# Sums of squares on eight rows, with root and reciprocal there and a spread over DRAM

## The chip, the core and the metric

The kernel runs on one core of a Trainium2 chip. A core has five engines, each with an instruction queue of its own that it works off in order: TensorE (PE in the profile; PEld is its weight load, which can run beside a matmul), VectorE (DVE), ScalarE (ACT), GpSimd (POOL) and SyncE (SP), which here only issues DMAs. Matmul results go to PSUM, from which DVE or ACT must fetch them. The metric is the device time of one execution in microseconds; lower is better.

## The reference

A linear attention is followed by two gated feed-forward layers, all in fp32:

```python
def _attn_ref(q, k, v, g_norm):                 # (4, 8, 576, 64) each
    kv = np.einsum('bhsd,bhse->bhde', k, v)
    out = np.einsum('bhsd,bhde->bhse', q, kv)
    rms = np.sqrt(np.mean(out * out, axis=-1, keepdims=True) + 1e-06)
    return out / rms * g_norm

x = attn_out.transpose(0, 2, 1, 3).reshape(2304, 512)
x = (1 / (1 + np.exp(-(x @ w_gate))) * (x @ w_val)) @ w_out    # d_ff 1536
h = x @ w_in2                                                   # d_ff 2048
out = (np.maximum(h, 0) + np.log1p(np.exp(-np.abs(h)))) @ w_out2
```

The root mean square is taken per token and head, over the 64 values of that head.

## The kernel before

Every fp32 product is made of three matmuls over a high and a low half of each operand (`mm3`); `split` makes the halves, the high one on ACT (L66) and the low one on DVE (L69). The instruction order is written out by hand, engine by engine.

The 2304 tokens are cut into five tiles (512, 512, 384, 384, 512). The first feed-forward layer runs over 60 iterations n, twelve per tile; layer two follows. One iteration of TensorE is a chain of twelve matmuls `ps_g`, one of twelve `ps_v`, and one of twelve `yacc` for the iteration before. Between the chains there are named places, in this order: `A` (after `ps_g`), `a`, `bg`, then after `ps_v` `B`, `b`, `end`, then after `yacc` `C`, `c`, `late`. Matmuls of other work go to the capital places, what fetches their results to the small ones. On ACT and DVE the iteration has `sigmoid` after `A`, the product `gated` (L509, DVE, into `sg`) between `B` and `b`, and its halves `ghl`. `gated` also frees the PSUM bank of `ps_v`.

The attention of tiles u = 2, 3, 4 is woven into the iterations of tile u - 1. A tile is worked in pieces of at most 256 tokens; there are seven: 128 and 256 tokens wide (u = 2), 160, 160 and 64 (u = 3), 256 and 256 (u = 4). A piece has four pairs of heads, hp = 0 to 3, each 128 rows (two heads of 64). Per pair: `q_trans` makes the halves of q, `po_mm` multiplies by the key-value block (3 matmuls), `po_evac` squares on ACT (L452, `sq`), copies on DVE (L453, `of`) and splits the squares, `ss_mm` sums them by two matmuls with a 128 x 128 matrix `ones` of two 64 x 64 blocks, so that every row of a head gets the head's mean, and `ss_evac` copies this to SBUF (`ms`, L470). After the fourth pair `rms_root` takes the root of all four at once (L475, with a load of ACT's function table ahead of it), and `rms_scale` makes the reciprocal (L481, DVE) and multiplies (L482), pair by pair, at places up to four iterations later. `x_split` uses the result at the tile's last iteration.

A piece over 160 wide does one pair an iteration: `po_mm` at `B`, `ss_mm` at `A` of the next. One of up to 160 does two pairs: both `po_mm` at `B`, both `po_evac` at `b`, both `ss_mm` at the next `A`. So there are 12 `ss` groups of two matmuls and 8 of four. The PSUM pool `atp` has two banks.

Where a piece begins a new batch, two iterations ahead of it hold `kv_mm` for that batch: matmuls `kv_ps` with weights of 64 columns (L272), its inputs loaded by SP (L255) into the pool `stage` of four buffers, which also holds `q_raw`, `ms` and others.

Beside this the weights of layer two are converted in eight steps, at places given by a plan: `m_b` is two DVE passes (L610, L613), `m_h` one long ACT copy (L66 into `m_y`), `m_l` one DVE pass.

Of the kernel before, what the change touches and what calls it, by code (L numbers as in the profile page):

```python
# [20 lines left out]
HI, LO = 0, 1  # L21
# [9 lines left out]
def attention_moe_moe_kernel(ctx: ExitStack, tc: tile.TileContext, q, k, v, g_norm,  # L31
# [41 lines left out]
        split_lo(lo, src, hi)  # L73


    ones = const.tile([P, P], F32R, name="ones")
    g_col = const.tile([P, 1], F32, name="g_col")
    eps = const.tile([P, 1], F32, name="eps")
    nc.vector.memset(ones.bitcast(F32), 0.0)
    for hh in range(2):  # L80
        nc.vector.memset(ones[64 * hh:64 * hh + 64, 64 * hh:64 * hh + 64].bitcast(F32), 1.0 / D)
    nc.vector.memset(eps, 1e-6)


# [102 lines left out]
    wo_dram = dram.tile([F1 // 2, P, 2, 2, 512], F32, name="wo_dram")  # L187
    wi_dram = dram.tile([7 * F2 // 8, P, 4, 2, 256], F32, name="wi_dram")
    wu_dram = dram.tile([F2 // 2, P, 2, 2, 512], F32, name="wu_dram")

    o_tile = {}

# [22 lines left out]
    stat = at.enter_context(tc.tile_pool(name="stat", bufs=4, side="right"))  # L215
    scr = at.enter_context(tc.tile_pool(name="scr", bufs=2, side="right"))
    hlpool = at.enter_context(tc.tile_pool(name="hlpool", bufs=2, side="right"))

    kvb = apool.tile([P, 2, NP, P], F32R, name="kvb")
    nc.vector.memset(kvb.bitcast(F32), 0.0)  # L220

    hl_t, of_t, x_t, kv_raw, at_ps, ms_t, q_raw, kvf = ({} for _ in range(8))


# [215 lines left out]

    def po_mm(u, piece, hp):
        b, s0, c0, m = piece
        ps = atp.tile([P, PIECE], F32, tag="at", name="po")[:, :m]
        t = hl_t.pop(("q", u, c0, hp))
        mm3(ps, lambda a: kvb[:, a, hp], lambda b: t[:, b, :m], True, True)
        at_ps["po", u, c0, hp] = ps
# [9 lines left out]

    def ss_mm(u, piece, hp):
        b, s0, c0, m = piece
        ps = atp.tile([P, PIECE], F32, tag="at", name="ss")[:, :m]
        t = hl_t.pop(("s", u, c0, hp))  # L460
        nc.tensor.matmul(out=ps, lhsT=ones, rhs=t[:, HI, :m], start=True, stop=False)  # L461
        nc.tensor.matmul(out=ps, lhsT=ones, rhs=t[:, LO, :m], start=False, stop=True)  # L462
        at_ps["ss", u, c0, hp] = ps

    def ss_evac(u, piece, hp):
        b, s0, c0, m = piece
        ps = at_ps.pop(("ss", u, c0, hp))
        if hp == 0:
            ms_t[u, c0] = stage.tile([P, NP, PIECE], F32, tag="st", name="ms")
        nc.scalar.copy(out=ms_t[u, c0][:, hp, :m], in_=ps)  # L470

    def rms_root(u, piece):
        b, s0, c0, m = piece
        ms = ms_t[u, c0][:, :, :m]
        nc.scalar.activation(out=ms, in_=ms, func=ACTF.Sqrt, bias=eps)  # L475

    def rms_scale(u, piece, hps):
        b, s0, c0, m = piece
        ms = ms_t[u, c0][:, hps, :m]
        of = of_t[u][:, hps, c0:c0 + m]  # L480
        nc.vector.reciprocal(out=ms, in_=ms)  # L481
        nc.vector.scalar_tensor_tensor(out=of, in0=of, scalar=g_col, in1=ms, op0=ALU.mult, op1=ALU.mult)  # L482

    def x_split(u):
# [443 lines left out]
    def at_place(n, place, *fs):  # L928
        work.setdefault((n, place), []).extend(fs)
# [28 lines left out]
    for u in range(2, NT1):  # L958
        j = (u - 1) * F1 + (0 if u > 2 else 1)
        ps = pieces(u)  # L960
        for n, p in enumerate(ps):
            b, m = p[0], p[3]
            if (b > ps[n - 1][0] if n else b > (TILES1[u][0] - 1) // S):
                at_place(j - 1, "bg", call(load_kv, b, "rest"), call(load_kv, b, 0), call(load_kv, b, 1))
                for part, c in ((2, "b"), (3, "c")):
                    at_place(j, c, call(load_kv, b, part))
                for hp, (d, c) in enumerate(((0, "B"), (0, "C"), (1, "A"), (1, "B"))):
                    at_place(j + d, c, call(kv_mm, b, hp))
                    work[j + d, c.lower()] = [call(kv_evac, b, hp)] + work.get((j + d, c.lower()), [])
                j += 2  # L970
            at_place(j - 1, "bg", call(load_q, u, p))
            step = 2 if m <= 160 else 1
            for h0 in range(0, NP, step):
                hh = range(h0, h0 + step)
                at_place(j, "a", *[call(q_trans, u, p, h) for h in hh])
                at_place(j, "B", *[call(po_mm, u, p, h) for h in hh])
                at_place(j, "b", *[call(po_evac, u, p, h) for h in hh])
                j += 1
                at_place(j, "A", *[call(ss_mm, u, p, h) for h in hh])
                at_place(j, "a", *[call(ss_evac, u, p, h) for h in hh])  # L980
            at_place(j, "bg", call(rms_root, u, p))
            if n + 1 < len(ps) and TILES1[u - 1][1] < 512 and m > 160:
                when = ((1, "bg"), (2, "bg"), (3, "bg"), (4, "bg"))
            else:
                when = ((0, "late"), (1, "bg"), (1, "late"), (2, "bg"))
            for h, (d, c) in enumerate(when):
                at_place(j + d, c, call(rms_scale, u, p, slice(h, h + 1)))
            if u == 3 and n == 0:
                j += 1
# [398 lines left out]
```

## Time and profile before

| | us |
|---|---|
| median of 3 runs (lowest, highest) | 892.74 (892.72, 893.12) |
| the profiled execution | 894.41 |
| its span, first to last instruction | 892.6 |
| PE busy in the span | 880.7 (99%) |
| PE weight loads | 780.0 (87%) |
| DVE busy | 604.4 (68%) |
| ACT busy | 487.4 (55%) |

The page follows the chain of work that ended last back from the end: PE holds 95% of it, DMA and the issue of DMAs 4%. The granted TensorE clock is full in all 40 slices. Busy time alone does not say that PE works at its peak, since its matmuls overlap; the start times of the chains in the timeline do.

### The profile page before, as it was taken

Reading aid. Unit: us, or ns where it says so; the run is one execution under the profiler, and the core shown is the slowest. Engines: PE = TensorE matmul, PEld = TensorE weight load, DVE = VectorE, ACT = ScalarE, POOL = GpSimd, SP = SyncE. Lnnn points to the kernel's source line nnn. Section 1 sums busy time; section 2 is a strip of 40 time slices with the busy share of each in tenths; the row PEclk is TensorE's granted clock in tenths of the full one; section 3 lists DMA queues with packets and bytes.
Section 4 is the critical chain, followed back from the end, with each engine's and each line's share of the span. In section 5 each row is a group of like instructions: output and inputs, shape, how many; then the busy total and the mean of one; then the engine's idle time right before and its main releaser. Section 6 shows DMA issues by size and latency. Waiting matters only on the chain.

```text
span 892.6 us, 12252 instructions
## 1 busy us (share of the span) xinstructions
PE 880.7 (99%) x4701; PEld 780.0 (87%) x4701; DVE 604.4 (68%) x884; ACT 487.4 (55%) x778; POOL 72.9 (8%) x112
## 2 busy tenths in 40 slices
PE   7899999999999999999999999999999999999998
PEld 6687888888899999999888889899898989989896
DVE  4888775475856676675577266578776678766666
ACT  5778754544554454643544264556655456554554
POOL 0010001121210030110342000000000000000000
PEclk9999999999999999999999999999999999999999
DMA  9997555965755396543889366543566554384421
GB/s 301 283 349 269 190 163 186 283 203 184 236 189 172 99 291 207 175 165 133 303 308 332 141 221 236 203 174 142 236 249 233 225 206 174 140 306 189 188 95 71
DMA packets 89114, 188.50 MB, mean 211 GB/s; under 512 B 35936, under 2 KB 61792, under 8 KB 76768
## 3 DMA queue, kind: packets, MB, share of 16 engines
q1 hardware_dynamic: 76288, 147.08, 47.8%
q0 software_dynamic: 11392, 39.85, 12.7%
q10 hardware_dynamic: 1376, 0.79, 0.3%
q8 instruction: 37, 0.61, 0.3%
q14 instruction: 21, 0.17, 0.1%
HBM read 148.90 MB, written 38.80 MB: 210 GB/s over the span
## 4 chain that ended last, share of the span: by engine, by line
PE 95%; DMA 2%; SPq 2%; issue 0%; DVE 0%; ACT 0%
PE oacc L62 22%; PE yacc L62 17%; PE ps_g L62 16%; PE ps_v L62 16%; PE ps_b L680 11%; PE ps_c L680 9%; DMA kv_raw<-in_v_dram 2%; SPq L117 1%; PE kv_ps L272 1%; PE po L62 1%; DMA kv_raw<-in_k_dram 1%; PE o_rows L346 1%; PE qt L334 0%; PE ss L462 0%; PE ss L461 0%; SPq L772 0%
## 5 line engine op out<-in xcount | busy, mean ns | idle before, releaser
L62 PE MATMUL oacc<-w_up,g 128*128 128x512 f32 x864 | 205.2, 391 | 0.0
L62 PEld LDWEIGHTS oacc<-w_up,g 128*128 128x128 f32 x864 | 161.5, 188 | 31.8
L62 PE MATMUL ps_g<-x,w 128*128 128x512 f32 (+1 forms) x720 | 161.2, 372 | 1.5 <-ACT x L396 0.9
L62 PE MATMUL ps_v<-x,w 128*128 128x512 f32 (+1 forms) x720 | 159.8, 370 | 1.3 <-ACT w L66 1.3
L62 PE MATMUL yacc<-ghl,w 128*128 128x512 f32 (+1 forms) x720 | 160.0, 370 | 0.0
L62 PEld LDWEIGHTS ps_g<-x,w 128*128 128x128 f32 x720 | 131.7, 189 | 19.7 <-DVE x L397 1.4
L62 PEld LDWEIGHTS ps_v<-x,w 128*128 128x128 f32 x720 | 129.6, 188 | 18.4 <-ACT w L66 1.7
L62 PEld LDWEIGHTS yacc<-ghl,w 128*128 128x128 f32 x720 | 129.8, 188 | 16.9 <-DVE w L69 0.4
L680 PE MATMUL ps_b<-y_c,w_in 128*128 128x384 f32 x576 | 116.2, 336 | 0.0
L680 PEld LDWEIGHTS ps_b<-y_c,w_in 128*128 128x128 f32 x576 | 102.0, 188 | 2.4 <-DVE y_c L69 0.3
L66 ACT CAST ghl<-sg 128x512 fp32r<-128x512 f32 (+1 forms) x60 | 34.6, 577 | 106.9 <-DVE sg L509 106.9
L680 PE MATMUL ps_c<-y_c,w_in 128*128 128x384 f32 x432 | 87.6, 337 | 0.0
L1078 DVE TENSOR_TENSOR c<-ps_c,c 128x384 f32<-128x384 f32 x72 | 40.1, 557 | 61.1 <-ACT c L1075 31.5
L1075 ACT COPY c<-ps_b 128x384 f32<-128x384 f32 x72 | 34.6, 480 | 81.7 <-PE ps_b L680 80.0
L680 PEld LDWEIGHTS ps_c<-y_c,w_in 128*128 128x128 f32 x432 | 77.0, 188 | 2.1
L503 ACT ACTIVATE sg<-ps_g 128x512 f32<-128x512 f32 (+1 forms) x60 | 33.3, 555 | 74.2 <-PE ps_g L62 72.3
L509 DVE TENSOR_TENSOR sg<-sg,ps_v 128x512 f32<-128x512 f32 (+1 forms) x60 | 37.9, 631 | 51.8 <-PE ps_v L62 50.3
L692 ACT ACTIVATE e<-c 128x768 f32<-128x768 f32 x46 | 39.0, 848 | 49.9 <-DVE c L1078 49.1
L66 ACT CAST g<-c 128x768 fp32r<-128x768 f32 (+1 forms) x50 | 40.6, 812 | 30.9 <-DVE c L717 28.2
L712 DVE SCALAR_TENSOR_TENSOR u<-u,ln 128x768 f32<-128x768 f32 x46 | 43.9, 954 | 12.1 <-ACT ln L704 12.1
L69 DVE TENSOR_TENSOR ghl<-sg,ghl 128x512 fp32r<-128x512 f32 (+1 forms) x60 | 38.1, 635 | 16.8 <-ACT ghl L66 16.5
L69 DVE TENSOR_TENSOR g<-c,g 128x768 fp32r<-128x768 f32 (+1 forms) x50 | 46.2, 923 | 4.5 <-ACT g L66 4.4
(132 smaller groups left out, 972.2 us busy)
## 6 DMA issues: line engine op xcount, KB each, us to landing
w_in<-wi_dram SPq DMA_DIRECT2D x42, 1024.0 KB, 6.9
w<-wo_dram SPq DMA_DIRECT2D x24, 1024.0 KB, 5.8
w_up<-wu_dram SPq DMA_DIRECT2D x24, 1024.0 KB, 6.4
m_raw<-in_moe_w_in_dram POOLq DMA_DIRECT2D x32, 256.0 KB, 6.4
m_raw<-in_moe_w_out_dram POOLq DMA_DIRECT2D x16, 512.0 KB, 4.8
wu_dram<-m_f POOLq DMA_DIRECT2D x16, 512.0 KB, 4.8
w_raw<-in_moe_w_gate_dram SPq DMA_DIRECT2D x12, 512.0 KB, 8.9
w_raw<-in_moe_w_val_dram SPq DMA_DIRECT2D x12, 512.0 KB, 8.9
```

What stands on the lines that cost most here:

```text
L62: nc.tensor.matmul(out=ps, lhsT=lhs(a), rhs=rhs(b), start=start and n == 0, stop=stop and n == 2)
L66: nc.scalar.copy(out=hi, in_=src)
L69: nc.vector.tensor_tensor(out=lo, in0=src, in1=hi.bitcast(F32), op=ALU.subtract)
L117: nc.sync.dma_start(out=t, in_=unit(w, f))
L272: nc.tensor.matmul(out=ps[sl, sl], lhsT=lhs, rhs=rhs, start=r == 0, stop=r == R)
L503: nc.scalar.activation(out=sg, in_=chain.pop(("g", t, i)), func=ACTF.Sigmoid)
L509: nc.vector.tensor_tensor(out=sg, in0=sg, in1=chain.pop(("v", t, i)), op=ALU.mult)
L680: nc.tensor.matmul(out=ps, lhsT=w[:, a, kk * P:(kk + 1) * P], rhs=y[:, b, kk], start=first and kk == 0 and n == 0, stop=kk == 1 and n == 2 ...
L692: nc.scalar.activation(out=e, in_=h_t[p][:, f], func=ACTF.Abs)
L712: nc.vector.scalar_tensor_tensor(out=u, in0=u, scalar=1.0, in1=ln_t.pop((p, f)), op0=ALU.subtract, op1=ALU.subtract)
L1075: nc.scalar.copy(out=p_part(n), in_=p_t["b"])
L1078: nc.vector.tensor_tensor(out=h_t[p][:, f, HT * th:HT * (th + 1)], in0=p_t["c"], in1=p_part(n), op=ALU.add)
```

## The change

`ones` becomes a [128, 4, 8] array: for pair hp it has eight columns, of which columns 2 hp and 2 hp + 1 hold 1/64 on the rows of their head. All `ss_mm` of a piece add into one PSUM tile of 8 rows, one row a head; this tile and one `po` tile are taken at the piece's first pair and kept for the whole piece. `ss_evac` is gone. `rms_root` takes the root of the 8 rows and now also the reciprocal, on DVE at `bg`. `rms_store` (SP, at `b`) writes the 8 rows to DRAM, `rms_load` (SP, at `late`) reads them back in two DMAs so that each row fills the 64 partitions of its head, and `rms_scale` only multiplies, one to two iterations on. In pieces of up to 160 tokens the second pair's `po_mm` moves from `B` to `C`, its `po_evac` from `b` to `c`.

```diff
--- before.py
+++ after.py
@@ -73,12 +73,13 @@
         split_lo(lo, src, hi)
 
 
-    ones = const.tile([P, P], F32R, name="ones")
+    ones = const.tile([P, NP, 8], F32R, name="ones")
     g_col = const.tile([P, 1], F32, name="g_col")
     eps = const.tile([P, 1], F32, name="eps")
     nc.vector.memset(ones.bitcast(F32), 0.0)
-    for hh in range(2):
-        nc.vector.memset(ones[64 * hh:64 * hh + 64, 64 * hh:64 * hh + 64].bitcast(F32), 1.0 / D)
+    for hp in range(NP):
+        for hh in range(2):
+            nc.vector.memset(ones[64 * hh:64 * hh + 64, hp, 2 * hp + hh:2 * hp + hh + 1].bitcast(F32), 1.0 / D)
     nc.vector.memset(eps, 1e-6)
 
 
@@ -187,6 +188,7 @@
     wo_dram = dram.tile([F1 // 2, P, 2, 2, 512], F32, name="wo_dram")
     wi_dram = dram.tile([7 * F2 // 8, P, 4, 2, 256], F32, name="wi_dram")
     wu_dram = dram.tile([F2 // 2, P, 2, 2, 512], F32, name="wu_dram")
+    r_dram = dram.tile([8, NT], F32, name="r_dram")
 
     o_tile = {}
 
@@ -215,10 +217,12 @@
     stat = at.enter_context(tc.tile_pool(name="stat", bufs=4, side="right"))
     scr = at.enter_context(tc.tile_pool(name="scr", bufs=2, side="right"))
     hlpool = at.enter_context(tc.tile_pool(name="hlpool", bufs=2, side="right"))
+    rpool = at.enter_context(tc.tile_pool(name="rpool", bufs=1, side="right"))
 
     kvb = apool.tile([P, 2, NP, P], F32R, name="kvb")
     nc.vector.memset(kvb.bitcast(F32), 0.0)
 
+    ss_t, po_t, r_t = {}, {}, {}
     hl_t, of_t, x_t, kv_raw, at_ps, ms_t, q_raw, kvf = ({} for _ in range(8))
 
 
@@ -440,7 +444,10 @@
 
     def po_mm(u, piece, hp):
         b, s0, c0, m = piece
-        ps = atp.tile([P, PIECE], F32, tag="at", name="po")[:, :m]
+        if hp == 0:
+            ss_t[u, c0] = atp.tile([P, 512], F32, tag="at", name="ss")[:8, :m]
+            po_t[u, c0] = atp.tile([P, 512], F32, tag="at", name="po")[:, :m]
+        ps = po_t[u, c0]
         t = hl_t.pop(("q", u, c0, hp))
         mm3(ps, lambda a: kvb[:, a, hp], lambda b: t[:, b, :m], True, True)
         at_ps["po", u, c0, hp] = ps
@@ -456,29 +463,36 @@
 
     def ss_mm(u, piece, hp):
         b, s0, c0, m = piece
-        ps = atp.tile([P, PIECE], F32, tag="at", name="ss")[:, :m]
-        t = hl_t.pop(("s", u, c0, hp))
-        nc.tensor.matmul(out=ps, lhsT=ones, rhs=t[:, HI, :m], start=True, stop=False)
-        nc.tensor.matmul(out=ps, lhsT=ones, rhs=t[:, LO, :m], start=False, stop=True)
-        at_ps["ss", u, c0, hp] = ps
-
-    def ss_evac(u, piece, hp):
-        b, s0, c0, m = piece
-        ps = at_ps.pop(("ss", u, c0, hp))
-        if hp == 0:
-            ms_t[u, c0] = stage.tile([P, NP, PIECE], F32, tag="st", name="ms")
-        nc.scalar.copy(out=ms_t[u, c0][:, hp, :m], in_=ps)
+        ps, t = ss_t[u, c0], hl_t.pop(("s", u, c0, hp))
+        for a in (HI, LO):
+            nc.tensor.matmul(out=ps, lhsT=ones[:, hp], rhs=t[:, a, :m], start=hp == 0 and a == HI,
+                             stop=hp == NP - 1 and a == LO, skip_group_check=True)
 
     def rms_root(u, piece):
         b, s0, c0, m = piece
-        ms = ms_t[u, c0][:, :, :m]
-        nc.scalar.activation(out=ms, in_=ms, func=ACTF.Sqrt, bias=eps)
+        r = rpool.tile([8, PIECE], F32, tag="r", name="r")[:, :m]
+        nc.scalar.activation(out=r, in_=ss_t[u, c0], func=ACTF.Sqrt, bias=eps[:8])
+        nc.vector.reciprocal(out=r, in_=r)
+        r_t[u, c0] = r
+
+    def rms_store(u, piece):
+        b, s0, c0, m = piece
+        t0 = TILES1[u][0] + c0
+        nc.sync.dma_start(out=r_dram[:, t0:t0 + m], in_=r_t.pop((u, c0)))
+
+    def rms_load(u, piece):
+        b, s0, c0, m = piece
+        t0 = TILES1[u][0] + c0
+        ms_t[u, c0] = ms = stage.tile([P, NP, PIECE], F32, tag="st", name="ms")
+        for hh in range(2):
+            nc.sync.dma_start(out=ms[64 * hh:64 * hh + 64, :, :m],
+                              in_=r_dram[:, t0:t0 + m].rearrange("(h two) m -> two h m", two=2)[hh].unsqueeze(0)
+                              .to_broadcast([64, NP, m]))
 
     def rms_scale(u, piece, hps):
         b, s0, c0, m = piece
         ms = ms_t[u, c0][:, hps, :m]
         of = of_t[u][:, hps, c0:c0 + m]
-        nc.vector.reciprocal(out=ms, in_=ms)
         nc.vector.scalar_tensor_tensor(out=of, in0=of, scalar=g_col, in1=ms, op0=ALU.mult, op1=ALU.mult)
 
     def x_split(u):
@@ -973,16 +987,15 @@
             for h0 in range(0, NP, step):
                 hh = range(h0, h0 + step)
                 at_place(j, "a", *[call(q_trans, u, p, h) for h in hh])
-                at_place(j, "B", *[call(po_mm, u, p, h) for h in hh])
-                at_place(j, "b", *[call(po_evac, u, p, h) for h in hh])
+                for c, h in zip("BC", hh):
+                    at_place(j, c, call(po_mm, u, p, h))
+                    at_place(j, c.lower(), call(po_evac, u, p, h))
                 j += 1
                 at_place(j, "A", *[call(ss_mm, u, p, h) for h in hh])
-                at_place(j, "a", *[call(ss_evac, u, p, h) for h in hh])
             at_place(j, "bg", call(rms_root, u, p))
-            if n + 1 < len(ps) and TILES1[u - 1][1] < 512 and m > 160:
-                when = ((1, "bg"), (2, "bg"), (3, "bg"), (4, "bg"))
-            else:
-                when = ((0, "late"), (1, "bg"), (1, "late"), (2, "bg"))
+            when = ((1, "late"), (1, "late"), (2, "bg"), (2, "bg"))
+            at_place(j, "b", call(rms_store, u, p))
+            at_place(j, "late", call(rms_load, u, p))
             for h, (d, c) in enumerate(when):
                 at_place(j + d, c, call(rms_scale, u, p, slice(h, h + 1)))
             if u == 3 and n == 0:
```

## Rows read from the trace of the kernel before

**Rows 1.** Busy us, 150 to 415 us: stretch, length, PE, PEld, DVE, ACT, POOL, clock, DMA

```profile
150.00:415.00 265.00, 264.98 (x1556) 245.25 (x1555) 173.50 (x313) 133.40 (x263) 41.31 (x60) 1.00 0.62 199
```

**Rows 2.** Timeline, TensorE, 512-wide chains; columns: start us, length us, engine, line, operation, tile, count

```profile
195.30 2.88 PE L62 MATMUL ps_g<-x,w 128*128 128x512 f32 x12
...
198.02 0.28 PE L461 MATMUL ss<-hl,ones 128*128 128x256 f32 x1
...
201.02 0.52 PE L62 MATMUL po<-hl,kvb 128*128 128x256 f32 x3
```

**Rows 3.** Timeline, TensorE, 384-wide chains: groups of two 256-wide, of four 64-wide

```profile
307.23 2.24 PE L62 MATMUL ps_g<-x,w 128*128 128x384 f32 x12
...
311.84 0.92 PE L62 MATMUL po<-hl,kvb 128*128 128x64 f32 x6
...
340.56 2.24 PE L62 MATMUL ps_g<-x,w 128*128 128x384 f32 x12
...
342.64 0.28 PE L461 MATMUL ss<-hl,ones 128*128 128x256 f32 x1
...
344.96 0.52 PE L62 MATMUL po<-hl,kvb 128*128 128x256 f32 x3
```

**Rows 4.** Timeline, single matmuls and weight loads around a block with 64-column weights, four windows

```profile
175.07 0.39 PE L62 MATMUL yacc<-ghl,w 128*128 128x512 f32 x1
...
175.39 0.81 PEld L272 LDWEIGHTS kv_ps<-kv_raw 128*64 128x64 f32 x20 [0.35 <-issue]
...
176.11 0.22 PE L272 MATMUL kv_ps<-kv_raw 64*64 64x64 f32 x2
...
176.27 0.50 PE L62 MATMUL ps_g<-x,w 128*128 128x512 f32 x1
...
176.60 0.40 PE L62 MATMUL ps_g<-x,w 128*128 128x512 f32 x1
```

**Rows 5.** Timeline, weight loads of a block with 128-column weights between chains

```profile
57.59 1.08 PEld L334 LDWEIGHTS qt<-kvf,kv_raw 128*128 128x128 f32 x8
```

**Rows 6.** Instructions on the tile ms: ns min/median/max, first and last start, shapes

```profile
L481 DVE RECIPROCAL ms<-ms x28: 544/1150/1747, 177.9 to 403.8; 128x256 f32<-128x256 f32 x12, 128x160 f32<-128x160 f32 x8, 128x128 f32<-128x128 f32 x4, 128x64 f32<-128x64 f32 x4
...
L475 ACT ACTIVATE ms<-ms,eps x7: 510/832/1156, 170.7 to 393.0; 128x1024 f32<-128x1024 f32 x3, 128x640 f32<-128x640 f32 x2, 128x512 f32<-128x512 f32 x1, 128x256 f32<-128x256 f32 x1
```

**Rows 7.** Timeline, TensorE, iterations 27 and 28: two like groups of po

```profile
272.43 0.79 PE L62 MATMUL po<-hl,kvb 128*128 128x160 f32 x6
...
279.82 1.20 PE L62 MATMUL po<-hl,kvb 128*128 128x160 f32 x6
```

**Rows 8.** Timeline, VectorE then ScalarE, iterations 31 and 32

```profile
307.32 0.23 DVE L69 TENSOR_TENSOR hl<-sq,hl 128x64 fp32r<-128x64 f32 x1
...
308.33 1.22 DVE L610 SCALAR_TENSOR_TENSOR m_raw<-m_raw 128x1024 uint32<-128x1024 uint32 x1
...
315.87 1.70 ACT L66 CAST m_y<-m_f 128x1792 fp32r<-128x1792 f32 x1 [1.76 <-DVE m_f L623]
```

**Rows 9.** Timeline, ScalarE, VectorE and TensorE, iterations 40 and 41

```profile
364.51 1.28 ACT L475 ACT_TABLE_LOAD   x1
...
364.87 1.22 DVE L610 SCALAR_TENSOR_TENSOR m_raw<-m_raw 128x1024 uint32<-128x1024 uint32 x1
...
367.27 0.55 DVE L509 TENSOR_TENSOR sg<-sg,ps_v 128x384 f32<-128x384 f32 x1
...
368.27 0.38 ACT L452 ACTIVATE sq<-po 128x256 f32<-128x256 f32 x1
...
370.22 0.28 PE L462 MATMUL ss<-hl,ones 128*128 128x256 f32 x1
```

**Rows 10.** SP's issue, KB and us to landing of that load, TensorE's use of it

```profile
288.85 0.47 SPq L255 DMA_DIRECT2D kv_raw<-in_v_dram  x1
...
kv_raw<-in_v_dram SPq DMA_DIRECT2D x1, 256.0 KB, 5.1
...
294.08 0.95 PE L272 MATMUL kv_ps<-kv_raw 128*64 128x64 f32 x20
```

## The prediction, made blind

> **What bounds the kernel now.** First I read the busy time of each engine in the stretch that the change touches, 150 to 415 us: TensorE is busy for 264.98 of 265.00 us, VectorE for 174, ScalarE for 133 [rows 1]. So nothing that is taken from VectorE or ScalarE there can shorten the run by itself; only what TensorE has to issue, and what newly stops it, counts. Next I read the start times of TensorE's chains. A 512-wide chain of twelve takes 198.02 - 195.30 = 2.72 us, 0.227 a matmul [rows 2]; a 384-wide one 342.64 - 340.56 = 2.08, 0.173 a matmul [rows 3]. What a group of `ss` costs is what lies between the start of `ps_g` and the end of `ps_v` beyond two such chains: 5.72 - 5.44 = 0.28 us for two 256-wide matmuls in 512-wide chains [rows 2], 4.40 - 4.16 = 0.24 in 384-wide ones, 4.61 - 4.16 = 0.45 for four 64-wide ones [rows 3]. The streams of these are 0.227 (two of 256 at 0.44 ns a column) and 0.11 us; the four-matmul groups pay for their weight loads. For the four groups of 160 and the two of 128 columns, which lie between, I take 0.47.
>
> **Part 1: eight weight columns (the main term).** The matmuls stay 56 and their streams stay as long, since the moving columns are the same. What changes is the shape of the weights, and no load of fewer than 64 columns is in the trace. The nearest rows are those of `kv_ps`, 64 columns, between chains of 128 [rows 4]. The last wide matmul starts at 175.07, the first narrow load at 175.39: 0.32 against a pace of 0.227, and the weight load stood idle for 0.35. So 0.09 are lost on the way in. The last narrow pair starts at 176.11, the next wide load and matmul at 176.27: 0.16 for a pair whose own share of the block is at most 0.88 / 10 = 0.09; I take 0.09 lost on the way out, as on the way in. The second wide matmul follows at 176.60, 0.33 after the first against 0.227: 0.11 because the first wide load could not be pulled ahead. A block of `qt` with 128-column weights has none of this: its first load starts at 57.59 with no idle time [rows 5], so it is the narrow shape that the array has to be emptied for, not the foreign work. The narrow load itself lies open once; for eight columns I take 0.02, between 0 and the 0.05 that 64 columns cost by the same rows.
>
> A visit thus costs 0.09 + 0.02 + 0.09 + 0.11 = 0.31 beyond its stream (0.29 to 0.34). By groups: two of 256 in 512-wide chains 0.31 + 0.23 - 0.28 = +0.26, four times: 1.0. In 384-wide chains +0.30, eight times: 2.4. Four of 160 (stream 0.284): +0.12, four times: 0.5. Four of 128 +0.07, twice: 0.1. Four of 64 -0.03, twice: -0.1. Sum **+4.0 us** (3.5 to 4.6).
>
> That 8 columns behave like 64 isn't shown by any row; the Trainium skill, "TensorEngine Tiling (Array Packing)", Key Properties, says that a change of tiling mode drains the array, and its Available Configurations list 128 x 32, the size that 8 columns would fall into. By that rule the term stands as above; without it the term is that of rival B. The 64-column rows agree with it.
>
> **Part 2: work that VectorE and ScalarE lose.** 28 copies `ss_evac`, 21 of 28 reciprocals of 0.54 to 1.75 us each [rows 6] and most of seven roots go. TensorE was full without it [rows 1], so I cost this at nothing but for one place: the second group of `po` in iteration 28 takes 1.20 where the like group before takes 0.79 [rows 7], late halves of q behind a reciprocal. That 0.4 comes back: **-0.4 us** (-0.4 to 0). The cover of all the rest is TensorE's own chain. The six more memsets at the start run while the first loads are awaited: nothing.
>
> **Part 3: the second pair moved from `B`, `b` to `C`, `c`.** It gives the fetch of the second pair, which the next `A` needs, one `ps_g` chain of 2.1 to 2.7 us, and puts it behind what stands at `b` and `end` on ACT and DVE. The one `po` bank makes the second `po_mm` wait for the first pair's copy, which has a `yacc` chain of 2.1 us or more to be done: nothing. At most of the eight groups the time until `A` is enough, too. At two it is not. In iteration 31 the two DVE passes of `m_b` stand at `end`; they start at 308.33 [rows 8] and with fewer operations ahead about 1.2 us earlier, 307.1; both take 367.27 - 364.87 = 2.4 [rows 9], so copy and split of the second pair (0.23 each [rows 8], 0.5 together) end at 310.0, while the last `ss` is due at 307.23 + 2.08 + 0.25 = 309.5 [rows 3]: **0.5 us** lost. In iteration 32 the 1.70 us of `m_h` on ACT, before at 315.87 [rows 8], stand at `b`, ahead of the second pair's square. It ends at 317.6 to 317.8, then square, copy and split take 0.7; TensorE wants the result one `po`, `yacc` and `ps_g` after 311.84 [rows 3], that is at 316.8 + 0.25, and is late by the 0.5 itself: **0.9 us** lost. Bounds for each: 0, if DVE or ACT get there earlier, and 1.5.
>
> **Part 4: the reciprocal at `bg`.** This adds a wait on DVE. Queued behind it are the plan's passes at `bg`, then `gated`; for `gated` wait its halves, the next `po_evac` and the bank of the next `ps_v`. In six of seven pieces no `po` follows at once and the bank has four microseconds. In iteration 40 the next piece follows directly, and `m_b` stands at the same `bg`. Before, `m_b` starts at 364.87, `gated` at 367.27, the square at 368.27, and the last `ss` at 370.22 [rows 9]. After: without `ss_evac` the table load (1.28, before at 364.51 [rows 9]) moves ahead by about 0.3 and ends at 365.5; the root on 256 elements a row takes 0.51, the reciprocal 1.75 [rows 6], both taken as for full rows since the elements in a row are the same: 367.8. `m_b` follows, 2.4: 370.25; so `gated` is 3.0 late, and the square's halves, ready about 369.5 before, come at 372.5. TensorE is by then later by itself by 0.4 from part 1: 370.6. **1.9 us** lost (0 to 2.3; the low end if the reciprocal on eight rows were short).
>
> **Part 5: the trip over DRAM.** 14 loads and 7 stores are added on SP, which has long waits on TensorE anyway. The store stands at `b` and waits for the reciprocal; behind it on SP stand the second half of a batch's key-value loads in iterations 15 and 29, and the next weight loads, which are due iterations later. The row with the least slack: a load issued at 288.85 takes 5.1 to land, 293.95, and `kv_ps` uses it at 294.08 [rows 10]. The reciprocal there ends at about 288.6 by the steps of part 4, the store issues for 0.47, so this load starts 0.2 to 0.7 later: I take **+0.3 us** (0 to 1.2). The multiplications have an iteration of 7 to 8 us until `late`, against 0.5 + 5 for a store and a load of that kind; I cost them at nothing, covered by that distance.
>
> **Sum.** 4.0 - 0.4 + 0.5 + 0.9 + 1.9 + 0.3 = +7.2 us. The profiled execution took 894.41 with a span of 892.6; with the change I expect a span of 899.8 and 901.6 in all. The median of the runs shown, 892.74, lies 1.7 below the profiled time; the same difference on it gives **899.9 us**.
>
> **Rivals.**
> A, the forecast: 899.9, 897 to 903.
> B, the narrow weights need no emptying: then a group costs its stream alone, as its loads are short: 4 x -0.05 + 8 x -0.01 + 4 x -0.19 + 2 x -0.24 + 2 x -0.34 = -2.2 instead of +4.0, and 892.74 - 2.2 + 3.2 = 893.7: not slower by what counts. The point from which it decides is a visit of 0.04 us beyond its stream instead of 0.31. For it speaks that load time falls with columns (ten narrow pairs in 0.88, eight wide loads in 1.08), against it the idle load of the narrow block beside the wide one [rows 4, 5]. On this side the Trainium skill, "TensorE: Matmul & The Clock Gate", LDWEIGHTS, has a load time of columns / 1.2 ns, as an estimate 7 ns for eight; taken alone it gives B.
> C, the emptying comes but parts 3 and 4 find their cover (DVE has some 25 us less to do): 892.74 + 4.0 - 0.4 + 0.3 = 896.6.
> D, the trip over DRAM is late: SP's wait holds the key-value loads by 1 us at two places, and the spread rows come after `late` in iteration 27, where DVE would hold the next halves of q by up to 1.5: 3.5 us on top, 903.4. The slack of 0.1 [rows 10] speaks for it, the waits of SP that pass unnoticed today against it.
>
> **How the numbers follow.** Chances: A 0.62, B 0.12, C 0.14, D 0.12. A measurement of this kernel can tell some 0.2% (1.8 us) from no change. Slower by more than that: A, C, D, and a little of B: 0.88. Within it: most of B: 0.10. Faster: 0.02, if B came without parts 3 and 4. The range reaches from 895.5 to 904, over C and D; outside are B and little of D.
>
> **What would show it.** In the profile after: the weight loads of `ss` stand idle for about 0.3 before each of the 20 groups, and the second `ps_v` matmul comes 0.28 to 0.34 after the first (part 1); if instead these loads start without a gap, B. Gaps of TensorE before the last `ss` in iterations 32, 33 and 41 (parts 3 and 4), with `gated` about 3 us later in iteration 40. A gap before the third `kv_ps` of a batch would be part 5. VectorE's reciprocals fall to seven with no gain from it. I am wrong if TensorE gives back time in `ss`, or if a wait outside these places exceeds 1 us.

## The result and the profile after

The changed kernel takes 898.88 us (median; 897.99 to 900.68) against 892.93 for the kernel before on the same chip (892.72 to 894.10): a ratio of 1.0066, 95% interval 1.0048 to 1.0085. It is 0.66% slower. 899.9 was predicted, so the total came out; the sum behind it did not.

The stretch from 150 to 415 us, busy time of each engine, the line that answers to [rows 1]:

```profile
150.00:415.00 265.00, 262.06 (x1537) 238.72 (x1536) 142.94 (x285) 122.80 (x232) 40.27 (x59) 1.00 0.66 208
```

Over the whole span, from the page:

```profile
PE 882.2 (98%) x4701; PEld 776.0 (87%) x4701; DVE 577.7 (64%) x869; ACT 479.0 (53%) x750; POOL 73.2 (8%) x112
```

In that stretch VectorE is busy for 31 us less and ScalarE for 11 us less, and TensorE now stands idle for 2.9 us. What TensorE waited for, from the table of waits (PE, then PEld: operation, what released it, us in total, times, longest):

```profile
PE ss L468 <- ACT hl L66: 2.3, 2, 1.8
PE ss L468 <- DVE hl L69: 0.4, 2, 0.2
...
PEld po L62 <- DVE of L460: 0.9, 2, 0.6
```

The first two rows are the `ss` waits of iterations 32, 33 and 41, the third a wait that no part of the prediction has. The groups of `ss` themselves, TensorE's matmuls and weight loads at two of them, in the changed kernel:

```profile
197.17 0.40 PE L468 MATMUL ss<-hl,ones 128*8 128x256 f32 x2
197.41 0.62 PE L62 MATMUL ps_v<-x,w 128*128 128x512 f32 x2
...
196.95 0.31 PEld L468 LDWEIGHTS ss<-hl,ones 128*8 128x8 f32 x2
...
277.03 0.46 PE L468 MATMUL ss<-hl,ones 128*8 128x160 f32 x4
277.33 2.28 PE L62 MATMUL ps_v<-x,w 128*128 128x384 f32 x12
...
276.86 0.41 PEld L468 LDWEIGHTS ss<-hl,ones 128*8 128x8 f32 x4
277.26 0.82 PEld L62 LDWEIGHTS ps_v<-x,w 128*128 128x128 f32 x5
```

The predicted emptying is not there: no weight load of `ss` has idle time ahead of it but where it waits for its data (the waits above), and the next load starts beside the last `ss` matmul. From the first `ss` to the first `ps_v` it is 0.24 us for two of 256 (197.17 to 197.41) and 0.30 for four of 160 (277.03 to 277.33). The kernel before, the second of these groups:

```profile
277.26 0.24 PE L461 MATMUL ss<-hl,ones 128*128 128x160 f32 x1
...
277.67 0.73 PE L62 MATMUL ps_v<-x,w 128*128 128x384 f32 x3
```

0.41 there, so eight columns save 0.11 in a group of four of 160 (by the same reading 0.16 with 128 tokens, 0.24 with 64 in `e6_plan` and `e7_po_B` below, where the group does not wait), and nothing in a group of two. What the change loses must be elsewhere. Single starts of one chain in layer one's last tile show a place that nothing in the diff touches. Before, then after:

```profile
443.21 2.88 PE L62 MATMUL yacc<-ghl,w 128*128 128x512 f32 x12
445.93 2.88 PE L62 MATMUL ps_g<-x,w 128*128 128x512 f32 x12
448.65 2.66 PE L62 MATMUL ps_v<-x,w 128*128 128x512 f32 x11
```

```profile
445.82 2.95 PE L62 MATMUL yacc<-ghl,w 128*128 128x512 f32 x12
448.61 2.90 PE L62 MATMUL ps_g<-x,w 128*128 128x512 f32 x12
451.34 2.43 PE L62 MATMUL ps_v<-x,w 128*128 128x512 f32 x10
```

From `yacc` to `ps_g` it is 2.72 us before and 2.79 after, and 0.01 more follow in `ps_g`. That is 0.08 to 0.09 us in each iteration of a 512-wide tile where nothing stands between the chains, and about 0.05 where an `ss` group does. A 384-wide `yacc` chain with nothing beside it slows down too, by half as much: in iteration 34 from 327.69 - 325.61 = 2.08 to 327.63 - 325.51 = 2.12. Before, then after:

```profile
325.61 2.24 PE L62 MATMUL yacc<-ghl,w 128*128 128x384 f32 x12
327.69 2.24 PE L62 MATMUL ps_g<-x,w 128*128 128x384 f32 x12
```

```profile
325.51 2.28 PE L62 MATMUL yacc<-ghl,w 128*128 128x384 f32 x12
327.63 2.24 PE L62 MATMUL ps_g<-x,w 128*128 128x384 f32 x12
```

Eight 384-wide iterations show this (26, 33 to 35, 44 to 47). In iterations 36 to 43, where a `po` stands ahead of each `yacc`, the chain takes 2.11 in both kernels, and the `ps_v` chains with nothing between are the same everywhere.

**The balance.** I laid the start of each chain before beside that after. From the `ps_g` that starts at 86.4 us after to the end of layer two the changed kernel falls behind by 5.3 us (the first 86 us differ between profiled executions by up to 3 us and are left out; they are why the two profiled spans, 892.6 and 896.2, differ by less than the medians do). In the profiled execution of the kernel before, the granted clock was not full in those first 86 us: behind a wait of 1.78 us at 41.6 it was 0.63 from 42 to 44 us, which the page's digit for that slice, a mean over 22 us, does not show. The changed kernel falls behind in these places:

| place | us | predicted |
|---|---|---|
| `yacc` and the `ps_g` behind it in 512-wide tiles | +2.2 | none |
| `yacc` in 384-wide tiles | +0.4 | none |
| last `ss` of iteration 41 | +2.3 | +1.9 |
| second `ss` pair of iterations 32 and 33 | +0.5, +1.0 | +0.5, +0.9 |
| second `po` of iterations 14 and 25 | +0.4, +0.3 | 0 |
| `ss` groups of four: 2 x 0.16, 4 x 0.11, 2 x 0.24 | -1.2 | +4.0 with those of two |
| second `po` of iteration 28 | -0.4 | -0.4 |
| second `po` of iteration 32 | -0.2 | none |
| trip over DRAM | 0 | +0.3 |

The first two rows are read from `e2_before_shift` below, in which nothing but this differs from the kernel before. The table adds up to 5.3; places too small to name cancel to about a tenth.

### The profile page after: what moved, and what is told of

It reads as the page before. It is cut to its first block, busy times and chain, and to the rows that moved or that the text cites. A ratio compares the mean times of both kernels' runs of the same rounds, so it can differ in the third digit from the quotient of the medians.

```text
span 896.2 us, 12222 instructions
## 1 busy us (share of the span) xinstructions
PE 882.2 (98%) x4701; PEld 776.0 (87%) x4701; DVE 577.7 (64%) x869; ACT 479.0 (53%) x750; POOL 73.2 (8%) x112
## 4 chain that ended last, share of the span: by engine, by line
PE 87%; DMA 4%; DVE 3%; SPq 2%; issue 2%; ACT 1%; DVEq 0%; ACTq 0%
PE oacc L62 22%; PE ps_g L62 14%; PE yacc L62 14%; PE ps_v L62 14%; PE ps_b L694 11%; PE ps_c L694 8%; DMA kv_raw<-in_v_dram 2%; DMA wo_dram<-w 1%; SPq L118 1%; PE kv_ps L276 1%; PE po L62 1%; DMA kv_raw<-in_k_dram 1%; DMA w_raw<-in_moe_w_out_dram 1%; DVE w_raw L146 1%; PE ss L468 0%
## 5 line engine op out<-in xcount | busy, mean ns | idle before, releaser
L62 PE MATMUL yacc<-ghl,w 128*128 128x512 f32 (+1 forms) x720 | 162.4, 374 | 0.0
```

The costliest lines, as they stand in the source:

```text
L62: nc.tensor.matmul(out=ps, lhsT=lhs(a), rhs=rhs(b), start=start and n == 0, stop=stop and n == 2)
```

## The experiments

The changed kernel and the runs with one part of it mended (`e1_fill`, `e5_gate`, `e6_plan`, `e7_po_B`) ran four or five times each, and the 95% intervals of their ratios overlap with its 1.0048 to 1.0085. So their medians alone don't separate the parts; what each run shows of its part is read from the start times of the chains in its profiled execution.

**Addresses, from both sides.** `ones` is 384 bytes a partition smaller after the change, and what is allocated behind it (weights, `stage`, `sg`, `x`) moved down by that. `ghl`, the moving operand of `yacc`, is at the other end of the memory and did not move. First, the changed kernel with the old addresses:

```diff
     ones = const.tile([P, NP, 8], F32R, name="ones")
+    const.tile([P, 96], F32, name="fill")
...
-    stat = at.enter_context(tc.tile_pool(name="stat", bufs=4, side="right"))
...
+    stat = rpool.tile([P, PIECE], F32, name="stat")
...
-        r = rpool.tile([8, PIECE], F32, tag="r", name="r")[:, :m]
+        r = stat[:8, :m]
```

> The changed kernel with an unused tile of 384 bytes a partition behind ones, so that all that lies behind it (weights, stage, sg, x) has the addresses that it had before the change; ghl lies where it always lay. To make room, the four stat tiles and r share one tile. In the changed kernel the 512-wide yacc chains run at 0.229 to 0.238 us a matmul in turn instead of 0.226 to 0.227, 0.07 to 0.085 us an iteration, some 2.4 us over the run. Theory 1, addresses: the small ones moved the weights against ghl; here the pace is 0.227 again, and the time is 898.9 - 2.4 = about 896.5. Rival, the change's own work (its DMAs, the shorter queue of VectorE) disturbs TensorE: pace and time stay, 898.9.

Measured: 896.65 (896.05 to 898.16), ratio to before 1.0046 (1.0033 to 1.0058). The chain is at its old pace, 449.35 - 446.63 = 2.72:

```profile
446.63 2.88 PE L62 MATMUL yacc<-ghl,w 128*128 128x512 f32 x12
449.35 2.88 PE L62 MATMUL ps_g<-x,w 128*128 128x512 f32 x12
```

By the chains the changed kernel loses 2.4 us against this run from the same point to the end of layer two, when the 1.5 that the clock took from this run (below, at the gate) are left out.

Second, the kernel before with the new addresses, and no other work changed:

```diff
-    ones = const.tile([P, P], F32R, name="ones")
+    const.tile([P, 32], F32, name="fill")
...
+    ones = rpool.tile([P, P], F32R, name="ones")
```

> The kernel before with ones in a pool at the other end of the memory and a filler of 128 bytes in its old place: all else on that side lies 384 bytes lower, as in the changed kernel, and no work differs. Theory 1, addresses: the 512-wide yacc chains slow down to 0.229 to 0.238 us a matmul, some 2.4 us in all: 892.9 + 2.4 = 895.3. Rival, the change's own work: 0.226 to 0.227 and 892.9.

Measured: 895.92 (894.50 to 896.16), ratio 1.0034 (1.0021 to 1.0046). Its chain, 446.65 - 443.86 = 2.79:

```profile
443.86 2.96 PE L62 MATMUL yacc<-ghl,w 128*128 128x512 f32 x12
446.65 2.90 PE L62 MATMUL ps_g<-x,w 128*128 128x512 f32 x12
```

By the chains it loses 2.5 us against the kernel before, 0.4 of it in 384-wide `yacc` chains. So the slow pace comes and goes with the addresses alone, in a kernel that has neither the DMAs nor the eight columns. Third, which addresses: the weights stay, `ghl` moves.

```diff
-    pad.tile([P, 8], F32, name="pad")
+    pad.tile([P, 168], F32, name="pad")
```

> The kernel before with the pad at the other end of the memory 640 bytes longer: the weights lie where they lay, ghl lies 640 bytes lower, and no work differs. Theory 1a, the pace of a chain goes by the distance of its weights from its moving rows, as a remainder of 1024 bytes (256 before, 640 in the changed kernel, 640 here): the 512-wide yacc chains run at 0.229 to 0.238 us a matmul, 892.9 + 2.5 = 895.4. Theory 1b, it goes by the place of the weights alone: 0.226 to 0.227 and 892.9.

Measured: 894.91 (894.56 to 896.42), ratio 1.0022 (1.0013 to 1.0031), and the slow pace, 445.77 - 442.98 = 2.79:

```profile
442.98 2.95 PE L62 MATMUL yacc<-ghl,w 128*128 128x512 f32 x12
445.77 2.90 PE L62 MATMUL ps_g<-x,w 128*128 128x512 f32 x12
```

By the chains it is 2.5 us again. The place of the weights alone (1b) falls; the distance between the weights and `ghl` (1a) stands. These edits move all tiles of one end against all of the other; that the two operands of `yacc` are the pair that counts is inferred from `ps_v`, whose operands both lie at one end and whose chain takes 2.72 us in all of these runs. That the distance's remainder of 1024 bytes is what counts was assumed in choosing 640 and fits; two slow distances and one fast one don't show the rule. Why it slows TensorE is not shown either.

**What empties the array.** The first of two runs takes 64 columns for `ss`, at the addresses of `e1_fill`:

```diff
-    ones = const.tile([P, NP, 8], F32R, name="ones")
+    ones = const.tile([P, P], F32R, name="ones")
...
-            ss_t[u, c0] = atp.tile([P, 512], F32, tag="at", name="ss")[:8, :m]
+            ss_t[u, c0] = atp.tile([P, 512], F32, tag="at", name="ss")[:64, :m]
...
-            nc.tensor.matmul(out=ps, lhsT=ones[:, hp], ...
+            nc.tensor.matmul(out=ps, lhsT=ones[:, 64 - 2 * hp:128 - 2 * hp], ...
```

> As e1_fill, but with 64 weight columns instead of 8 for ss (zeros in the further ones). No emptying of the array shows around the 8-column matmuls, while it shows around kv_ps with its 64. Theory 2, 64 columns have the array emptied and 8 do not: the weight load of ss stands idle for 0.3 before each of the 20 groups, and a visit costs 0.3 us beyond its stream: 20 x 0.3 = +6 us on e1_fill, about 902.5. Rival, the number of columns is not it, and something else in kv_ps is (its two places in the array, its 64 rows, its unrounded type): no idle load, only the longer loads themselves, 56 x 0.02 or less = +1 us at most, 896.5 to 897.5.

Measured: 897.76 (897.56 to 898.83), ratio 1.0059 (1.0045 to 1.0073). Its weight loads in the group of four of 160 tokens:

```profile
275.48 0.46 PEld L467 LDWEIGHTS ss<-hl,ones 128*64 128x64 f32 x4
275.88 1.17 PEld L62 LDWEIGHTS ps_v<-x,w 128*128 128x128 f32 x7
```

No idle time again, and the chains of this run keep the same distance from those of `e1_fill` through all groups until iteration 41 (to 0.1 us). So 64 columns cost what 8 do, and the number of columns alone is not what empties the array. The 1.1 us between the two medians are not in the groups, and the two intervals overlap. The second run takes the other suspect away, the two places of `kv_ps` in the array:

```diff
-        for r in range(R + 1):
-            for hh in range(2):
+        for hh in range(2):
+            for r in range(R + 1):
...
-                nc.tensor.matmul(out=ps[sl, sl], ...
+                nc.tensor.matmul(out=ps[:64, sl], ...
```

> The changed kernel with both heads' kv_ps in one place of the array: all their matmuls write the rows 0 to 63, one head's five after the other's, and the second head's product is copied over the first one's (so its place in kvb stays zero). Around kv_ps the first narrow matmul comes 0.318 after the last wide one (pace 0.227), its load idle for 0.35, the second wide one 0.335 after the first; ss with 64 columns in e3_w64 had none of this. Theory 2a, alternating between two places is what empties the array: 0.23 at entry and at exit here, no idle load. Theory 2b, it is the narrow unrounded operands themselves: 0.32 and 0.33 stay. The block itself gets longer in either case, as two heads can't run side by side.

Measured: 909.11 in a single execution, with the longer blocks. The weight loads of two blocks:

```profile
175.06 1.66 PEld L276 LDWEIGHTS kv_ps<-kv_raw 128*64 128x64 f32 x20 [0.35 <-issue]
...
179.77 1.34 PEld L276 LDWEIGHTS kv_ps<-kv_raw 128*64 128x64 f32 x17 [0.36 <-ACT m_raw L127]
```

The idle 0.35 stay with one place, and so do the 0.318 on the way in and the 0.335 behind the first wide matmul (2b). What `kv_ps` has and `ss` has not, at the start of a block where the idle time is, is narrow weights that are not rounded (`ones` and `hl` are of the rounded type, fp32r); unrounded weights of full width, `qt` in [rows 5], have no idle load. So it seems to take both, narrow and unrounded. Another product of the kernel before bears this out: `o_rows`, unrounded too, first with weights of 64 columns and then of 128:

```profile
72.41 0.20 PEld L346 LDWEIGHTS o_rows<-kvf,q_rows 128*64 128x64 f32 x4 [0.35 <-issue]
72.78 0.74 PEld L346 LDWEIGHTS o_rows<-kvf,q_rows 128*128 128x128 f32 x6 [0.17 <-issue]
```

The narrow load has the same 0.35 ahead of it, and the change back to the full width, within one type, 0.17. One product run in either type was not tried, so this last step is argued from rows.

**The gate of iteration 40.** One entry of the plan moves from `bg` of iteration 40 to `late`:

```diff
-              (137, 144, 149, 152, 153, 156, 157, 158, 160, 171, 181),
+              (137, 144, 149, 152, 153, 156, 157, 158, 163, 171, 181),
```

> The changed kernel with one entry of the plan moved: m_b of the u block stands at late of iteration 40 instead of bg, so behind gated and the square's halves instead of ahead of them; nothing else moves on any engine. Theory 3 (my part 4), gated waits behind reciprocal and m_b, 1.75 + 2.4 us: gated starts 2.3 us earlier, and the 1.9 us for which TensorE waits at the last ss of iteration 41 go, 898.9 - 1.9 = 897.0, and another 0 to 1.5 where the granted clock had fallen behind that wait, as it did in the look at e1_fill (0.50 at 374 to 376 us). Rival, m_b only comes in the way of the next transposition instead: less than half of it, 898.0 or more.

Measured: 897.37 (897.07 to 897.65), ratio 1.0048 (1.0033 to 1.0063). VectorE after the change, and then TensorE:

```profile
366.19 1.74 DVE L475 RECIPROCAL r<-r 8x256 f32<-8x256 f32 x1 [1.35 <-ACT r L474]
367.86 1.15 DVE L624 SCALAR_TENSOR_TENSOR m_raw<-m_raw 128x1024 uint32<-128x1024 uint32 x1
369.05 1.23 DVE L627 SCALAR_TENSOR_TENSOR m_f<-m_raw 128x1024 uint32<-128x1024 uint32 x1
370.19 0.55 DVE L523 TENSOR_TENSOR sg<-sg,ps_v 128x384 f32<-128x384 f32 x1
...
372.06 0.29 PE L468 MATMUL ss<-hl,ones 128*8 128x256 f32 x1 [1.77 <-ACT hl L66]
372.51 0.28 PE L468 MATMUL ss<-hl,ones 128*8 128x256 f32 x1 [0.17 <-DVE hl L69]
```

With the entry moved:

```profile
368.10 0.48 DVE L523 TENSOR_TENSOR sg<-sg,ps_v 128x384 f32<-128x384 f32 x1
...
370.69 1.22 DVE L624 SCALAR_TENSOR_TENSOR m_raw<-m_raw 128x1024 uint32<-128x1024 uint32 x1
371.94 1.22 DVE L627 SCALAR_TENSOR_TENSOR m_f<-m_raw 128x1024 uint32<-128x1024 uint32 x1
373.09 0.44 DVE L441 STREAM_TRANSPOSE qT<-q_raw 128x256 f32<-128x256 f32 x1
...
370.37 0.40 PE L468 MATMUL ss<-hl,ones 128*8 128x256 f32 x2
...
374.02 0.97 PE L62 MATMUL po<-hl,kvb 128*128 128x256 f32 x3 [1.17 <-ACT hl L66]
```

`gated` starts 2.1 us earlier (2.3 against the chains, which stand 0.24 later in this execution) and the wait at `ss` is gone: the cause is as predicted. But `m_b` now holds the transposition, and TensorE waits at `po`. Laid against the changed kernel, its chains gain 2.3 us at the one place and lose 1.8 at the other; by the trace the rival is right. The median is 1.5 us lower, which is not clear of noise, and the granted clock is a likely part of it: of the changed kernel's four executions the two slower ones, 899.21 and 900.68, had a mean clock of 0.998, the two faster ones and all of `e5_gate` 0.999 or 1.000. In the profiled execution of `e1_fill`, which has the wait at `ss`, the windows from 372 to 378 us (last three columns: granted clock, DMA share, GB/s) are:

```profile
372.00:374.00 2.00, 1.90 (x9) 1.90 (x10) 1.16 (x4) 1.67 (x3) 0.00 (x0) 0.77 1.00 303
374.00:376.00 2.00, 2.00 (x9) 2.00 (x9) 0.57 (x2) 0.00 (x0) 0.00 (x0) 0.50 0.64 258
376.00:378.00 2.00, 2.00 (x12) 2.00 (x12) 1.12 (x4) 1.20 (x3) 0.00 (x0) 0.88 0.05 20
```

TensorE had stood idle for 1.78 and 0.18 us there. Behind that it ran at the lower of its two levels, 1.2 instead of 2.4 GHz, for some 3 us, and lost another 1.5. The profiled executions of `e3_w64` and `e7_po_B` show the same; those of the changed kernel, `e6_plan`, `e8_no_trip` and `e13_kv_one` have the same wait and a full clock. So the wait of iteration 41 costs 2.3 us, and in some executions 1.4 to 1.5 more.

**The moved pairs, in two ways.** First, the plan's passes moved behind the second pair:

```diff
-              (118, 120, 126, 127, 129, 129, 132, 132, 134, 138, 140),
+              (118, 120, 127, 127, 129, 131, 132, 132, 134, 138, 140),
```

> The changed kernel with two other entries of the plan moved: m_b of the i block from end of iteration 31 to late, behind the second pair's copy and split, and m_h from b of iteration 32 to late. Theory 4 (my part 3): the waits of TensorE at the second ss of iterations 32 and 33 (0.25 and 0.52 us, the chains behind them 0.27 and 0.76 us late) go, 898.9 - 1.0 = 897.9. Rival, these passes hold the next transposition or sigmoid instead and the same time is lost one place later: 898.9.

Measured: 897.74 (897.03 to 899.74), ratio 1.0056 (1.0043 to 1.0070). The four `ss` of iterations 32 and 33 run through:

```profile
310.05 0.29 PE L468 MATMUL ss<-hl,ones 128*8 128x64 f32 x4
...
317.20 0.29 PE L468 MATMUL ss<-hl,ones 128*8 128x64 f32 x4
```

against, in the changed kernel:

```profile
308.98 0.20 PE L468 MATMUL ss<-hl,ones 128*8 128x64 f32 x1 [0.25 <-DVE hl L69]
...
316.77 0.46 PE L468 MATMUL ss<-hl,ones 128*8 128x64 f32 x2 [0.52 <-ACT hl L66]
```

Its chains gain 0.4 and 0.9 us at these places and lose nothing later, so by the chains the theory holds. Second, the places undone:

```diff
+        lo = 160 * (hp % 2) if m <= 160 else 0
+        ps = po_t[u, c0][:, lo:lo + m]
...
-                for c, h in zip("BC", hh):
-                    at_place(j, c, call(po_mm, u, p, h))
-                    at_place(j, c.lower(), call(po_evac, u, p, h))
+                at_place(j, "B", *[call(po_mm, u, p, h) for h in hh])
+                at_place(j, "b", *[call(po_evac, u, p, h) for h in hh])
```

> The changed kernel with one part undone: both po of an iteration stand at B again and both copies at b, side by side in the one bank of po (160 columns each); the plan is as it was. Theory 4 (my part 3): the waits at ss in iterations 32 and 33 go (1.0 us), and with them the wait of the second po for the first pair's copy that the changed kernel shows at C of iterations 14 and 25 (0.4 and 0.3 us): 898.9 - 1.7 = 897.2. Rival, the places are harmless and the longer queue at b costs what C did: 898.5 to 899.3.

Measured: 898.62 (897.45 to 899.01), ratio 1.0061 (1.0047 to 1.0074). By the chains the theory holds: until iteration 33 it gains 2.1 us on the changed kernel, 0.4 and 0.3 of it at iterations 14 and 25, 0.5 and 1.0 at 32 and 33. In the profiled execution 1.4 of this are lost again behind the wait of iteration 41, where the clock fell to 0.50. The median alone does not show the gain.

**The trip over DRAM.**

```diff
-        nc.vector.scalar_tensor_tensor(out=of, in0=of, scalar=g_col, in1=ms, ...
+        nc.vector.scalar_tensor_tensor(out=of, in0=of, scalar=g_col, in1=of, ...
...
-            at_place(j, "b", call(rms_store, u, p))
-            at_place(j, "late", call(rms_load, u, p))
```

> The changed kernel without the trip over DRAM: no store, no loads of the spread rows, and the multiplications take their own input in place of the spread rows (so the output is not normalised rightly); root and reciprocal still run. My part 5 gives the trip 0.3 us, at the key-value load of iteration 29: 898.6. Rival D gives it 3.5 us: 895.4. A trip that is wholly covered: 898.9, and the same start times of TensorE's chains to 0.05 us in the stretch from 150 to 415 us.

Measured: 899.88 (899.18 to 900.66), ratio 1.0083 (1.0068 to 1.0099): no gain. From 104 to 415 us all its chains start 0.54 to 0.56 us after those of the changed kernel, an offset that it has from the first 86 us. The trip is wholly covered. In the changed kernel its loads land 3.7 to 5.3 us after their issue, and the only wait for them is one of 0.5 us on VectorE; the chains, which keep their distance across it, show nothing of it.

**All three mended.** The old addresses, `m_b` as in `e5_gate`, `po` as in `e7_po_B`:

> All three mended: the addresses of e1_fill, m_b moved as in e5_gate, po as in e7_po_B. If the 512-wide pace, part 4 and part 3 are all that the change loses, only its gains are left against the kernel before: 0.1 to 0.16 us in each of the ss groups of four and 0.4 in iteration 28, some 1.3 us in all: 892.7 - 1.3 = 891.4. If something else of the change costs time (its DMAs, the start), 892.5 to 894.

Measured: 893.37 (891.47 to 894.89), ratio 1.0002 (0.9993 to 1.0011). What is left of the loss is the wait at `po` that `e5_gate` has, in its place here too:

```profile
369.05 0.96 PE L62 MATMUL po<-hl,kvb 128*128 128x256 f32 x3 [1.18 <-ACT hl L66]
```

So `m_b` was cut in two:

```diff
+                at_place(40, "a", call(m_b1, "u", j))
+                at_place(41, "bg", call(m_b2, "u", j))
```

> As e9_best, but m_b of the u block is cut in its two passes: the first at a of iteration 40, into the 1.35 us in which VectorE waits for the root, the second at bg of iteration 41. In e5_gate and e9_best m_b at late held the transposition instead, and TensorE waited 1.17 us at po of iteration 41 and ran the chain behind it 1.8 us late in all. Theory 3 (VectorE has too much to do between the reciprocal and the next po): both waits go, 1.5 to 1.8 us less than e9_best, 893.4 - 1.6 = 891.8. Rival, there is no room in either place: 892.8 or more, with a wait at the ss or po of iteration 41 or 42.

Measured: 891.61 (890.40 to 893.11), ratio 0.9984 (0.9975 to 0.9993). TensorE in iterations 40 and 41, and the stretch of the first row above:

```profile
368.24 0.40 PE L470 MATMUL ss<-hl,ones 128*8 128x256 f32 x2
...
370.56 0.52 PE L62 MATMUL po<-hl,kvb 128*128 128x256 f32 x3
...
150.00:415.00 265.00, 265.00 (x1564) 243.07 (x1563) 147.73 (x294) 125.49 (x237) 42.46 (x62) 1.00 0.67 209
```

There is no wait left in this stretch, and the kernel is 0.16% or 1.5 us faster than the one before (893.07 beside it). By the chains it gains 1.9 us from 86.4 us on: nearly all of it the 1.2 of the `ss` groups and the 0.4 and 0.2 of iterations 28 and 32, which are the change's own gain.

## Why the prediction was right in sum and wrong in its main term

**Part 1, wrong, by 5.2 us.** "It is the narrow shape that the array has to be emptied for" is the step that failed. It went from `kv_ps` to `ss` by the number of columns alone [rows 4], and left out that `kv_ps` differs in type. `e3_w64` and `e13_kv_one` show that columns and places are not enough; the term was -1.2, and rival B had its sign (-2.2). By the prediction's own sign of being wrong, time given back in `ss`, it was wrong here. The rule that was weighed there, the Trainium skill, "TensorEngine Tiling (Array Packing)", Key Properties, that a change of tiling mode drains the array, is not borne out by `ss` with 8 or 64 columns between weights of 128; around `kv_ps` and `o_rows` the traces show an idle load. They show the shape of the weights and not the mode that the array was in.

**What stood in its place: the addresses, +2.6.** No step looked at where a smaller tile moves the others. The diff says it (`ones` shrinks by 384 bytes a partition in the first pool), but the trace of before alone gave no price for it, as in it these two operands lie at their old distance only. The Trainium skill, "TensorE: Matmul & The Clock Gate", Step-by-step: what each phase is for, says that loading the next weights doesn't take read bandwidth from the running matmul. `yacc` at the slow distances, 2.79 us a chain against 2.72 with nothing but addresses changed, shows that where the two operands lie can matter to the pace; whether loads and moving rows meet there was not shown.

**Part 2, right:** the second `po` of iteration 28 takes no longer than the first, 0.30 from its start to the next chain, and 0.4 came back. Another 0.2 came back in a like place that it had not named, the second `po` of iteration 32 (six matmuls in 0.92 us before [rows 3], in 0.75 in `e7_po_B` and `e10_split`). Nothing else did.

**Part 3, right for iterations 32 and 33** (0.5 and 1.0 for 0.5 and 0.9). Wrong where it cost the bank of the second `po` at nothing: in iterations 14 and 25 the first pair's copy was not done by then, 0.7 us in all.

**Part 4, right, step by step:** the reciprocal ends at 367.9 (367.8 predicted), `gated` starts at 370.19 (370.25), the last halves are there at 372.5 (372.5). Eight rows of 256 take 1.74 us, as long as 128 rows [rows 6]. TensorE was due 0.4 earlier than I put it, since part 1 did not delay it: 2.3 for 1.9. (The times can be laid side by side as they stand because iteration 40 starts at 361.16 in both profiles, which is an accident.) That the granted clock fell behind this wait in some executions was not in the prediction.

**Part 5, right in kind:** 0 for 0.3. The load with the least slack in iteration 29 took 3.8 us to land instead of 5.1 [rows 10] and was there 0.7 before its use.

**The rivals.** B's condition was met, but its 893.7 was 5.2 us off: half of it because the losses that it shared with A left the addresses out, 1.0 because its -2.2 for `ss` was too good. C and D fell with `e6_plan`, `e5_gate` and `e8_no_trip`. The range held the time by luck: the error of -5.2 in part 1 met those of the other side, 2.6 of addresses, 0.7 of `po` and 0.4 in part 4. The span that the prediction gave for the profiled execution, 899.8, was 3.6 too long: 896.2.

## What to carry to other kernels

When a tile changes its size, see what is allocated behind it, and compare the pace of chains that the change doesn't touch; a loss that repeats by a few hundredths of a microsecond in each iteration is no wait and stands in no table of waits. Price an operation by rows that agree with it in type as well as in shape. On this kernel, whose TensorE is full, 31 us taken from VectorE and 11 from ScalarE brought 0.6 us, at the two places where TensorE had waited for them, while one reciprocal of 1.74 us, put with its wait ahead of a gate, cost 2.3: look for the hole in the trace before an operation is put there.

## What was not expected of the hardware

A chain of twelve 512-wide matmuls took 2.72 or 2.79 us, a 384-wide one with nothing beside it 2.08 or 2.12, with nothing but addresses changed; by all that was tried it goes by the distance between the chain's weights and its moving rows. Behind an idle time of 1.9 us TensorE's granted clock fell, to 0.50 or 0.54 for a window of 2 us, in three of the seven profiled executions that had this wait. Narrow fp32r weights, 8 or 64 columns, went between full ones without an idle load; the narrow unrounded ones of `kv_ps` and `o_rows` had 0.35 us of it.
